# Values of a third token block by Strassen's scheme, and the projections of all blocks made ahead of the three value blocks

## The chip, the core and the metric

The kernel runs on one core of one Trainium2 chip. Its time is the device time of one execution in microseconds. The median of three runs of the kernel before is 831.18 us (830.96 to 831.95). One execution was also taken with the hardware profiler; all views of the profile below come from that one.

## The reference

A block over 2048 tokens of 640 features: layer norm, then on the normalised input both an attention with 32 heads of 20 features and a sliding window of 256 tokens, and a two-layer network with squared ReLU whose output gates the attention's through SiLU. Everything is float32.

```
def _A_ref(x, wqkv, wo):                      # S = 2048, D = 640, H = 32, Dh = 20, W = 256
    qkv = (x @ wqkv).reshape(B, S, 3, H, Dh) ...
    q, k, v = qkv[0], qkv[1], qkv[2]
    scores = einsum("bhqd,bhkd->bhqk", q, k) * Dh ** -0.5
    mask = (i - j >= 0) & (i - j < W)
    p = softmax(where(mask, scores, -1e9))
    o = einsum("bhqk,bhkd->bhqd", p, v)
    return o.reshape(B, S, D) @ wo
def _B_ref(x, w1, b1, w2, b2):                # F = 1536
    h = relu(x @ w1 + b1) ** 2
    return h @ w2 + b2
xn = layernorm(x)
return x + _A_ref(xn, wqkv, wo) * silu(_B_ref(xn, w1, b1, w2, b2))
```

## The kernel before, in words

**Two halves.** Every operand of a large product is kept as two tiles, a high part in the format that TensorE takes (`F32R`) and a low part, the rest. A product then costs three matmuls per chunk of 128: high by high, low by high, high by low. ScalarE (ACT) makes the high part with a copy, VectorE (DVE) or GpSimd (POOL) the low part with a subtraction; in the code the pair is `split`, lines L117 and L118, or `split_w`, L192 and L193.

**Two phases.** Phase 1 (from L428) works on `NB = 4` blocks of `BT = 512` tokens. For each block `b` it normalises x (`norm_jobs`: statistics L157 and L158, the root on ACT L161, four normalisations L166), turns it on TensorE (`transpose_chunks`, 20 transposes L181 into five banks of PSUM, each split into `xT[0][b]` and `xT[1][b]`, the high and the low part), makes the first 128 rows of q and k from it (`qk_group`, 15 matmuls of 512 columns each, L214; `qk_evac` splits the result into `shm` and `slo` and queues their stores to `k_d` and `q_d` in HBM), and makes the values v. The two halves of a block's xT are also copied out whole to `xs` in HBM (`spill_x`, L175), because phase 2 reads them from there again. Phase 2 (the loop `for s in range(steps)` near the end of the file) is attention head pair by head pair, with the remaining projections and the two-layer network filling TensorE between. It begins with the scores of pair 0 (`sps`, L650) on the tiles `ks` and `qs`, which `pair_loads` reads back from `k_d` and `q_d` (L570).

**Values in two ways.** `v_all(b)` makes v of a block directly: 2 halves of the features by 4 tiles of tokens by 15 matmuls of 320 columns, 120 in all (L239). `v_blocks(b)` makes it by Strassen's scheme (in Winograd's form) on pairs of token tiles: two rounds `r`, each with 54 matmuls of the same width (L362, L407, L417, L419), 108 in all. For that it needs sums of the weights, made once (`weight_sums`: four tiles t1 to t4, cut into halves by eight jobs in the list `more`, L302 on ACT and L303 on POOL), and per round sums of the tokens (`token_sum`, kinds k = 1 to 4, on POOL, tile `sx`; `token_round` splits each into `svh` on ACT, L336, and `svl` on DVE, L337). `first_rounds` prepares the first round. Before the change block 0 and block 1 go through `v_all`, blocks 2 and 3 through `v_blocks`.

**Leaving PSUM.** A round has four results. ACT copies a partial product into a tile `m` (L379, three buffers), DVE adds it to a second one and writes v into the tile `vt` (L384). `vt` has two buffers, and a block uses both, one for each half of the features; each is stored to `v_d` in HBM when its block is done, so the first result of the next block has to wait for the store of the block before.

**What sets the order.** Phase 1 is under a manual schedule: on each of the five engines the instructions stand in the order in which the code emits them, and each waits only for its own semaphores. All DMAs of the kernel but a last few are issued by SyncE (SP), in order, on one queue (q1 in the profile). They use eight semaphores in turn, so a DMA cannot be issued before the eighth one back has landed. `store_all` issues what has been collected in `stores`.

Of the kernel before, what the change touches and what calls it, by code (L numbers as in the profile page):

```python
# [24 lines left out]
NB = 4  # L25
# [41 lines left out]
def attn_mlp_kernel(ctx: ExitStack, tc, x, wqkv, wo, w1, b1, w2, b2, out):  # L67
# [74 lines left out]
    with tc.tile_pool(name="ph1v", bufs=2) as p1v, tc.tile_pool(name="ph1", bufs=2) as p1, tc.tile_pool(name="ph1x", bufs=4) as p1b, tc.tile_pool(name="ph1w", bufs=1) as p1w, tc.tile_pool(name="ph1t", bufs=2, space=PSUM) as p1t:  # L142
# [98 lines left out]
        def v_all(b, between=None, firsts=()):  # L241
            jobs = norm_jobs(b + 2) if b + 2 < NB else []
            for nh in range(2):
                if nh and between:
                    between()
                vt = p1v.tile([P, NP // 2, 4, 2, VW], F32, tag="vt", name="vt")
                nc.gpsimd.memset(vt[:, :, :, :, VW - 1:VW], 1.0)
                ahead = 4 if between and not nh else 1
                pss = []
                for t in range(4):  # L250
                    if t in (0, ahead) or t > ahead:
                        ts = range(t, max(t + 1, ahead))
                        for t_ in ts:
                            pss.append(po_.tile([P, BT], F32, tag="o", name="vps")[:, :HALF] if t_ == 3 < ahead else mm_bank([P, HALF], "vps"))
                        for cs in ((range(KC - 1), (KC - 1,)) if len(ts) > 1 else (range(KC),)):
                            for t_, ps in zip(ts, pss):
                                v_part(ps, b, t_, nh, [(xp, wp, c) for c in cs for xp, wp in ((0, 0), (1, 0))], first=not cs[0])
                        for t_, ps in zip(ts, pss):
                            v_part(ps, b, t_, nh, [(0, 1, c) for c in range(KC)], last=True)
                    if firsts and not nh and not t:  # L260
                        firsts[0]()
                    ps = pss.pop(0)
                    psv = ps.rearrange("p (a h d) -> p a h d", a=NP // 2, h=2)
                    dst = vt[:, :, t, :, :]
                    if t % 2:
                        nc.scalar.activation(dst[:, :, :, 0:DH], psv, AF.Copy)
                    else:
                        nc.vector.tensor_copy(dst[:, :, :, 0:DH], psv)
                    if not nh and 0 < t < len(firsts):
                        firsts[t]()  # L270
                    for _ in range(0 if between and not nh else 2 if between else 1):
                        if jobs:
                            jobs.pop(0)()
                    for _ in range(2 if more and b else 0):
                        more.pop(0)()
                    store_all()
                stores.append((v_d[:, nh * (NP // 2):(nh + 1) * (NP // 2), b, :], vt.rearrange("p a t h w -> p a (t h w)")))

        TOKENS = [(b, r) for b in range(2, NB) for r in range(2)]
        sv = [p1w.tile([P, n, P], F32R, name=f"sv{q}{k}") for q in "hl" for k, n in enumerate((2, 2, 3, 2))]  # L280
        sx, sums_t = {}, {}

# [28 lines left out]
        def token_sum(n, k):  # L311
# [2 lines left out]
            (h0, h1), (l0, l1) = [[f32(v) for v in vs] for vs in token_views(n)]  # L314
            one, two = slice(0, 2), slice(3, 5)
            x = sx[k] = p1w.tile([P, 3 if k == 3 else 2, P], F32, tag=f"sx{k}", name=f"sx{k}")
            add, sub = nc.gpsimd.tensor_add, nc.gpsimd.tensor_sub
            if k == 1:
                add(x, h1[:, one], h1[:, two])
                add(x, x, l1[:, one])  # L320
# [108 lines left out]
        with tc.manual_schedule(engines={E_.PE, E_.Activation, E_.DVE, E_.Pool, E_.SP}):  # L429
# [99 lines left out]
            for b in range(NB):  # L529
                def next_x():  # L530
                    if b + 1 < NB:
                        alloc_x(b + 1)
                        transpose_chunks(b + 1, xns)
                        xns.clear()
                        store_all()
                        spill_x(b + 1)

                if b == 0:
                    xns, raws = [], []
# [6 lines left out]

                    def loads1():
                        load_x(2)
                        spill_x(0)
                        nc.sync.dma_start(b1t, b1.rearrange("(c p) -> p c", p=P))  # L550
                        nc.sync.dma_start(b2t, b2.partition_broadcast(P))
                        ones_rows(0)
                        raws.extend(load_w(group_src(1, w), KC) for w in "qk")
                    v_all(b, next_x, [lambda: norm1(0, 4), lambda: None, loads1])
                    more.extend(weight_sums())
                    continue
                for w in "kq":
                    ps = mm_bank([P, BT], "qkps")
                    qk_group(w, b, ps)
                    qk_evac(w, b, ps)  # L560
                    if b == 2:
                        first_rounds(w == "q")
                next_x()
                if b == 2:
                    first_rounds(2)
                if b == NB - 1:
                    store_all()
                    for half in range(2):
                        for dst, src in pair_loads(0, half):
                            nc.sync.dma_start(dst, src)  # L570
                if b == 1:
                    v_all(b)
                    for k in (1, 2, 4, 3):
                        token_sum(0, k)
                else:
                    v_blocks(b)
            store_all()


# [942 lines left out]
```

## Time and profile before

| what | value |
| --- | --- |
| median of the runs | 831.18 us |
| the profiled execution | 831.43 us |
| its span in the profile | 829.7 us |
| busy: TensorE (PE), DVE, ACT, POOL | 99%, 55%, 51%, 44% of the span |
| block 0: values from, to | 18.71, 38.51 us, with the transposes of block 1 inside |
| block 1: q and k; transposes of block 2; values | 38.51; 45.37; 47.47 to 65.16 us |
| block 2: q and k; transposes of block 3; values | 65.16; 72.02; 74.12 to 90.04 us |
| block 3: q and k; values | 90.04; 96.87 to 112.79 us |
| phase 2 on TensorE | from 112.79 us |

A row of the timeline gives the start, the busy time, the engine, the line, the operation with its output and inputs, and how many instructions were merged into it; SPq is the queue of DMA issues on SP. Matmuls are pipelined, so the busy time of a merged row runs a little past the start of the next, and the time of one matmul is best taken from start to start. A row of the windows gives busy time and count of each engine, then the granted clock, the share of the DMA engines and their GB/s.

### The profile page before, as it was taken

How to read it: one execution, taken by the hardware profiler on the slowest of the kernel's cores; microseconds unless marked ns; L12 is line 12 of the kernel's file. 1: busy time of each engine (PE TensorE's matmuls, PEld its weight loads, DVE VectorE, ACT ScalarE, POOL GpSimd, SP SyncE). 2: the span in 40 equal slices, each digit the busy share in tenths (PEclk: the TensorE clock that was granted, in tenths of full speed). 3: DMA queues.
4: the chain of work that ended last, by engine and by line, in shares of the span. 5: the costliest groups of instructions: out<-in, count | busy, mean ns of one | idle time of the engine just before them, and what ended most of it. 6: DMA issues, size and time to landing. Idle time of an engine off the chain costs nothing.

```text
span 829.7 us, 24649 instructions
## 1 busy us (share of the span) xinstructions
PE 822.3 (99%) x10082; PEld 777.8 (94%) x10082; DVE 456.8 (55%) x1398; ACT 425.2 (51%) x760; POOL 361.6 (44%) x672
## 2 busy tenths in 40 slices
PE   8999999999999999999999999999999999999997
PEld 8999999998889999999999999999999999999997
DVE  7856447655577545445444476655455445246663
ACT  6253323556566754743753764844644744754221
POOL 5167900334343543543543543643533643542452
PEclk9999999999999999999999999999999999999999
DMA  6998578888798646446083545585275456345962
GB/s 238 317 396 332 175 205 268 244 274 263 246 312 275 163 149 183 125 160 175 22 262 129 132 118 175 148 245 174 51 241 160 128 186 216 94 132 193 371 264 80
DMA packets 88808, 166.36 MB, mean 201 GB/s; under 512 B 10232, under 2 KB 36472, under 8 KB 87672
## 3 DMA queue, kind: packets, MB, share of 16 engines
q1 hardware_dynamic: 88536, 164.63, 62.7%
q8 instruction: 79, 1.29, 0.7%
q14 instruction: 33, 0.27, 0.1%
q10 hardware_dynamic: 160, 0.16, 0.1%
HBM read 93.66 MB, written 70.52 MB: 198 GB/s over the span
## 4 chain that ended last, share of the span: by engine, by line
PE 97%; DVE 1%; ACT 1%; DMA 0%; issue 0%; ACTq 0%
PE yps L640 21%; PE hps L640 20%; PE qkps L640 14%; PE ops L731 10%; PE wops L800 9%; PE stps L690 5%; PE sps L650 5%; PE vps L239 4%; PE qkps L214 3%; PE vps L362 3%; PE tps L181 1%; PE vps L417 0%; PE vps L407 0%; DMA xt<-in_A_x_dram 0%; DVE st L157 0%; DVE w L1006 0%
## 5 line engine op out<-in xcount | busy, mean ns | idle before, releaser
L658 DVE CUSTOM_DVE_ANT_0 junk<-sps,mask 128x384 bf16<-128x384 f32 (+2 forms) x512 | 252.1, 530 | 256.6 <-PE sps L650 108.2
L696 ACT ACTIVATE p<-stps 128x768 f32<-128x768 f32 (+2 forms) x256 | 197.5, 771 | 248.9 <-PE stps L690 231.4
L697 POOL TENSOR_SCALAR_AFFINE_SELECT p<-p 128x256 f32<-128x256 f32 x256 | 107.8, 421 | 331.6 <-ACT p L696 329.1
L640 PE MATMUL yps<-w,hh 64*128 64x320 f32 x1536 | 225.1, 309 | 0.3 <-DVE ysb L1200 0.2
L640 PE MATMUL hps<-xb,w 64*128 64x256 f32 (+1 forms) x2100 | 210.9, 304 | 0.0
L640 PEld LDWEIGHTS hps<-xb,w 64*128 64x128 f32 x2100 | 196.8, 186 | 3.3 <-issue 2.7
L640 PEld LDWEIGHTS yps<-w,hh 64*128 64x128 f32 x1536 | 185.9, 185 | 3.6 <-issue 2.3
L640 PE MATMUL yps<-w,hl 64*128 64x320 f32 x768 | 175.7, 308 | 0.0
L650 PE MATMUL sps<-ks,qs 60*128 60x384 f32 (+2 forms) x512 | 129.6, 333 | 0.1
L690 PE MATMUL stps<-qs,ks 62*128 62x384 f32 (+2 forms) x512 | 127.3, 331 | 0.2 <-ACT p L696 0.2
L640 PEld LDWEIGHTS yps<-w,hl 64*128 64x128 f32 x768 | 117.8, 185 | 0.4 <-issue 0.4
L640 PE MATMUL qkps<-xT,wgqh 64*128 64x512 f32 x320 | 99.4, 391 | 0.0
L640 PE MATMUL qkps<-xT,wgkh 64*128 64x512 f32 x320 | 98.1, 391 | 0.0
L699 POOL TENSOR_SCALAR_AFFINE_SELECT p<-p 128x256 f32<-128x256 f32 x224 | 94.9, 424 | 0.0
L731 PE MATMUL ops<-p,vp 128*21 128x128 f32 (+1 forms) x2128 | 86.6, 311 | 0.0
L731 PEld LDWEIGHTS ops<-p,vp 128*21 128x21 f32 x2128 | 63.6, 101 | 21.1 <-issue 6.4
L690 PEld LDWEIGHTS stps<-qs,ks 62*128 62x128 f32 x512 | 82.1, 187 | 1.2 <-ACT p L696 0.6
L650 PEld LDWEIGHTS sps<-ks,qs 60*128 60x128 f32 x512 | 81.2, 185 | 2.1 <-DVE mt L658 0.5
L1170 POOL TENSOR_TENSOR hl<-sq,hh 128x512 fp32r<-128x512 f32 x48 | 62.6, 1303 | 16.2 <-ACT sq L1169 15.5
L800 PE MATMUL wops<-wo,oT 128*128 128x320 f32 (+2 forms) x384 | 62.0, 310 | 0.0
L640 PE MATMUL qkps<-xT,wgql 64*128 64x512 f32 x160 | 61.3, 390 | 0.0
L640 PE MATMUL qkps<-xT,wgkl 64*128 64x512 f32 x160 | 61.2, 392 | 0.0
(163 smaller groups left out, 1236.0 us busy)
## 6 DMA issues: line engine op xcount, KB each, us to landing
ks<-k_d SPq DMA_DIRECT2D x64, 240.0 KB
qs<-q_d SPq DMA_DIRECT2D x64, 240.0 KB
xb<-xs SPq DMA_DIRECT2D x60, 256.0 KB
k_d<-shm SPq DMA_DIRECT2D x20, 512.0 KB
q_d<-shm SPq DMA_DIRECT2D x20, 512.0 KB
xs<-xT SPq DMA_DIRECT2D x8, 1280.0 KB
y<-ysb SPq DMA_DIRECT2D x28, 320.0 KB
o<-osb SPq DMA_DIRECT2D x64, 128.0 KB
```

Source lines behind the costliest of these rows:

```text
L214: nc.tensor.matmul(ps, wt[:, c, :], xT[part][b][:, c * BT + t0:c * BT + t0 + n], start=m == 1, stop=m == 3 * KC)
L239: nc.tensor.matmul(ps, xT[xp][b][:, c * BT + t * P: c * BT + (t + 1) * P], wv[wp][:, c, nh * HALF:(nh + 1) * HALF], start=first and m == 0 ...
L640: return nc.tensor.matmul(out, a[r], b_[r], skip_group_check=True, **kw)
L650: nc.tensor.matmul(ss[hh][:, :nk], qs[i][o, q * P:(q + 1) * P], ks[i][o, k0 * P:k0 * P + nk], start=True, stop=True)
L658: nc.vector.tensor_tensor_reduce(out=junk[:, :nk], in0=ss[hh][:, :nk], in1=mask[:, 3 * P - nk:], scale=1.0, scalar=-3.0e38, op0=ALU.add, o ...
L690: nc.tensor.matmul(tps[:, hh, :n], ks[i][o, kb * P:(kb + 1) * P], qs[i][o, kb * P:kb * P + n], start=True, stop=True)
L696: nc.scalar.activation(p32[:, :, :n], tps[:, :, :n], AF.Exp, scale=SCALE)
L697: nc.gpsimd.affine_select(p32[:, :, 0:P], p32[:, :, 0:P], pattern=[[0, 2], [1, P]], compare_op=ALU.is_ge, fill=0.0, base=0, channel_multip ...
L699: nc.gpsimd.affine_select(p32[:, :, 2 * P:], p32[:, :, 2 * P:], pattern=[[0, 2], [-1, P]], compare_op=ALU.is_gt, fill=0.0, base=0, channel ...
L731: nc.tensor.matmul(ot[r0:r0 + VW, c0:c0 + len(part), :], vps[p][:, kb // 4, kb % 4, hh, :], pts[p, kb][:, hh, :].rearrange("p (t n) -> p t ...
L800: nc.tensor.matmul(ps, a, b_, start=j == 0, stop=j == n - 1)
L1170: nc.gpsimd.tensor_sub(hh[1][:, :BT], sq, f32(hh[0]))
```

## The change

Block 1's values are now made by `v_blocks` too, so the list of rounds, `TOKENS`, has six entries in place of four. The order of phase 1 becomes: q and k of block 1, transposes of block 2, q and k of block 2, transposes of block 3, q and k of block 3, and then `v_blocks` of blocks 1, 2 and 3 in a row. The normalisation of block 3 (`norm_jobs(3)`), which was spread over `v_all(1)`, now follows the transposes of block 2. The jobs that cut the weight sums, also spread over `v_all(1)`, are taken three at a time behind each evacuation of q or k. The token sums of kind 3 go from POOL to DVE; those of the first round stand between k and q of block 2. `spill_x` leaves its four places, and all four blocks' copies are issued together at the start of block 3. The reads of `ks` and `qs` for pair 0 come before the three value blocks and not before the last one.

```
@@ v_all
-                    for _ in range(2 if more and b else 0):
-                        more.pop(0)()
                     store_all()
@@
-        TOKENS = [(b, r) for b in range(2, NB) for r in range(2)]
+        TOKENS = [(b, r) for b in range(1, NB) for r in range(2)]
@@ token_sum
-            add, sub = nc.gpsimd.tensor_add, nc.gpsimd.tensor_sub
+            eng = nc.vector if k == 3 else nc.gpsimd
+            add, sub = eng.tensor_add, eng.tensor_sub
@@ the loop over blocks
                         transpose_chunks(b + 1, xns)
                         xns.clear()
                         store_all()
-                        spill_x(b + 1)
...
                         load_x(2)
-                        spill_x(0)
...
                     more.extend(weight_sums())
                     continue
+                if b == NB - 1:
+                    for b_ in range(NB):
+                        spill_x(b_)
                 for w in "kq":
                     ps = mm_bank([P, BT], "qkps")
                     qk_group(w, b, ps)
                     qk_evac(w, b, ps)
-                    if b == 2:
+                    for _ in range(min(3, len(more))):
+                        more.pop(0)()
+                    if b == 2 and w == "k":
+                        for k in (1, 2, 4, 3):
+                            token_sum(0, k)
+                    if b == NB - 1:
                         first_rounds(w == "q")
                 next_x()
-                if b == 2:
-                    first_rounds(2)
-                if b == NB - 1:
-                    store_all()
-                    for half in range(2):
-                        for dst, src in pair_loads(0, half):
-                            nc.sync.dma_start(dst, src)
                 if b == 1:
-                    v_all(b)
-                    for k in (1, 2, 4, 3):
-                        token_sum(0, k)
-                else:
-                    v_blocks(b)
+                    for job in norm_jobs(NB - 1):
+                        job()
+            first_rounds(2)
+            store_all()
+            for half in range(2):
+                for dst, src in pair_loads(0, half):
+                    nc.sync.dma_start(dst, src)
+            for b in range(1, NB):
+                v_blocks(b)
             store_all()
```

The change shifts the lines behind it by one or two (the cut on ACT is L302 before and L300 after, the addition into `vt` L384 and L383). Three places of the order, each as the engine's instructions stand, show what moves.

ACT from the evacuation of block 1's k and q to the transposed halves of block 2 (`shm` is the high part of k or q, `t1h` to `t3h` are cut weight sums, `xT_2` the high half of block 2); before:

```order
L117 ACTIVATE shm<-qkps 128x512 x2
L117 ACTIVATE xT_2_707<-tps 128x512 x5
L302 ACTIVATE t3h<-wvr_195 128x320 x2
L266 ACTIVATE vt<-vps 128x8x2x20
L302 ACTIVATE t1h<-wvr_194 128x320 x2
L302 ACTIVATE t2h<-wvr_194 128x320 x2
```

and now:

```order
L117 ACTIVATE shm<-qkps 128x512
L300 ACTIVATE t3h<-wvr_195 128x320 x2
L300 ACTIVATE t1h<-wvr_194 128x320
L117 ACTIVATE shm<-qkps 128x512
L300 ACTIVATE t1h<-wvr_194 128x320
L300 ACTIVATE t2h<-wvr_194 128x320 x2
L117 ACTIVATE xT_2_715<-tps 128x512 x5
```

Three cuts now stand between the evacuation of q and the five copies of block 2's halves, which came directly behind each other before.

DVE from the low halves of block 2 to those of block 3, now (`st`, `mv`, `rstd` and `xn` are the statistics and the normalised x of block 3, `slo` the low parts of block 2's k and q, `sx_819` the first round's token sum of kind 3); the statistics of the other three tiles are left out, and before, these lines stood between the additions and copies of block 1's values:

```order
L118 TENSOR_TENSOR xT_2_716<-tps,xT_2_715 128x512 x5
L157 BN_STATS st<-xt_0_639 128x6 x2
L158 BN_AGGR mv<-st 128x2
...
L162 RECIPROCAL rstd<-rstd 128x4
L166 TENSOR_SCALAR xn<-xt_0_639,mv,rstd 128x640
...
L166 TENSOR_SCALAR xn<-xt_3_645,mv,rstd 128x640
L118 TENSOR_TENSOR slo<-qkps,shm 128x512
L325 TENSOR_TENSOR sx_819<-xT_1_505 128x384
L326 TENSOR_TENSOR sx_819<-sx_819,xT_1_506 128x384
L327 TENSOR_TENSOR sx_819<-sx_819,xT_1_506 128x384
L118 TENSOR_TENSOR slo<-qkps,shm 128x512
L118 TENSOR_TENSOR xT_3_844<-tps,xT_3_843 128x512 x5
```

The whole normalisation of block 3 stands between the halves of block 2 and the evacuation of block 2's k, and three token sums between the evacuations of k and q.

SP from the last store of block 2's q to the first stores of v, now (`xs` are the copies of x, `ks` and `qs` the reads for pair 0; rows that repeat for the other half are left out):

```order
L206 DMA q_d<-slo 128x512
L175 DMA xs_0_72<-xT_0_182 128x2560
L175 DMA xs_0_76<-xT_0_183 128x2560
...
L175 DMA xs_3_75<-xT_3_843 128x2560
L175 DMA xs_3_79<-xT_3_844 128x2560
L206 DMA k_d<-shm 128x2x512
...
L206 DMA q_d<-slo 128x512
L576 DMA ks_117<-k_d 60x1024
...
L576 DMA qs_116<-q_d 60x1024
L206 DMA v_d<-vt 128x8x168 x6
```

Before, two of the eight `xs` copies stood in each block's turn, and the stores of v of a block came ahead of the next block's q and k.

## The prediction

> **What bounds the kernel now.** I read the page's busy times first, then the chain that ended last, then TensorE's timeline over the stage that the change rewrites.
>
> ```profile
> span 829.7 us, 24649 instructions
> PE 822.3 (99%) x10082; PEld 777.8 (94%) x10082; DVE 456.8 (55%) x1398; ACT 425.2 (51%) x760; POOL 361.6 (44%) x672
> PE 97%; DVE 1%; ACT 1%; DMA 0%; issue 0%; ACTq 0%
> ```
>
> TensorE is the bound, with almost no idle time: 97% of the chain is its own work. A matmul taken away is worth its time, and every wait that TensorE gets is added in full, since nothing later is idle that could absorb it. So the stage decides.
>
> ```profile
> 45.37 2.34 PE L181 MATMUL tps<-ident,xn 128*128 128x128 f32 x20
> 47.47 17.85 PE L239 MATMUL vps<-wv,xT 128*128 128x320 f32 x120
> 65.16 1.33 PE L214 MATMUL qkps<-xT,wgkh 128*128 128x512 f32 x5
> 66.33 1.32 PE L214 MATMUL qkps<-xT,wgkl 128*128 128x512 f32 x5
> 72.02 2.35 PE L181 MATMUL tps<-ident,xn 128*128 128x128 f32 x20
> 74.12 2.45 PE L362 MATMUL vps<-wv,xT 128*128 128x320 f32 x15
> 90.04 1.32 PE L214 MATMUL qkps<-xT,wgkh 128*128 128x512 f32 x5
> ```
>
> From start to start: 20 transposes 2.10 us (45.37 to 47.47), direct values of a block 17.69 (to 65.16), q and k 6.86 (to 72.02), Strassen values 15.92 (74.12 to 90.04). The reader should see the order as well: behind the transposes of block 2 stand 17.69 us of values of block 1, which need nothing new. That is the cover under which ACT and DVE finish block 2's halves, normalise block 3 and cut the weight sums, and under which the queue writes x out.
>
> **The gain.** 108 matmuls for 120, at 17.69 / 120 = 15.92 / 108 = 0.147 us each: 12 x 0.147 = 1.8 us off. It is all that the change removes from TensorE; transposes, q and k stay.
>
> **Term 1: the halves of block 2.** Now q and k of block 2 follow its transposes, so they wait for ACT's copies.
>
> ```profile
> 45.62 0.60 ACT L117 ACTIVATE shm<-qkps 128x512 fp32r<-128x512 f32 x1 [2.80 <-PE qkps L214]
> 46.11 2.55 ACT L117 ACTIVATE xT<-tps 128x512 fp32r<-128x512 f32 x5
> 52.63 1.50 ACT L302 ACTIVATE t1h<-wvr 128x320 fp32r<-128x320 f32 x2
> 54.01 1.51 ACT L302 ACTIVATE t2h<-wvr 128x320 fp32r<-128x320 f32 x2
> ```
>
> The five copies began 0.49 us behind the evacuation of q and ended at 48.66. Three cuts now stand in between, at (54.01 - 52.63) / 2 = 0.69 each, 2.1 us: the fifth copy ends at 50.75. The fifth matmul of k would start at 47.47 + 4 x 0.234 = 48.4 (0.234 is (66.33 - 65.16) / 5) and now starts at 50.8: a wait of 2.4 us, and q of block 2 ends at 47.47 + 6.86 + 2.4 = 56.7. The cuts before q's evacuation are hidden, as ACT idled 2.80 us there.
>
> **Term 2: the normalisation of block 3.** Its cover has shrunk from 17.69 us to the 6.86 of q and k, and it begins late.
>
> ```profile
> 46.86 3.07 DVE L118 TENSOR_TENSOR xT<-tps,xT 128x512 fp32r<-128x512 f32 x5
> 54.76 0.88 DVE L157 BATCH_NORM_STATS2 st<-xt 128x6 f32<-128x320 f32 x2
> 55.80 0.83 DVE L157 BATCH_NORM_STATS2 st<-xt 128x6 f32<-128x320 f32 x2
> 38.07 0.30 ACT L161 ACTIVATE rstd<-mv,eps 128x4 f32<-128x4 f32 x1 [3.33 <-DVE mv L158]
> 38.61 2.18 DVE L166 TENSOR_SCALAR xn<-xt,mv,rstd 128x640 f32<-128x640 f32 x4
> 61.88 1.63 DVE L166 TENSOR_SCALAR xn<-xt,mv,rstd 128x640 f32<-128x640 f32 x2
> L118 DVE TENSOR_TENSOR slo<-qkps,shm 128x512 fp32r<-128x512 f32 x6 | 4.1, 689 | 12.8 <-ACT shm L117 12.8
> L337 DVE TENSOR_TENSOR svl<-sx,svh 128x384 fp32r<-128x384 f32 x4 | 2.4, 588 | 0.5 <-ACT svh L336 0.5
> L337 DVE TENSOR_TENSOR svl<-sx,svh 128x256 fp32r<-128x256 f32 x12 | 9.4, 787 | 5.2 <-ACT svh L336 5.2
> 70.10 0.41 DVE L337 TENSOR_TENSOR svl<-sx,svh 128x256 fp32r<-128x256 f32 x1
> ```
>
> DVE's low halves of block 2 follow the copies by one subtraction: 50.75 + 0.7 = 51.45. Statistics of a tile take 55.80 - 54.76 = 1.04, of four 4.2: 55.6. Root and reciprocal take 0.55 (38.07 to 38.61): 56.15. Four normalisations take 2.2 us with POOL idle (the row at 38.61) and 2 x 1.63 = 3.3 with POOL busy (61.88): 58.3 to 59.4. TensorE has run out at 56.7. Its transposes can then go, but k of block 3 needs the PSUM bank that q of block 2 leaves, and that evacuation stands behind the one of k (0.69) and behind three token sums which are new on DVE. No row has them there; the nearest is the subtraction of the same width, 0.59, and for the dear end I add what POOL's company costs the narrower one, 0.787 against 0.41 at rest: 0.97. So 0.69 + 3 x 0.59 + 0.69 = 3.15, or 4.3: k of block 3 starts at 61.4 to 63.7, middle 62.5, where without waits it would start at 47.47 + 6.86 + 2.10 = 56.4. Terms 1 and 2 together: **6.1 us (5.0 to 7.3)**. The 20 transposes end by 61.5 and lie inside this; so do block 3's copies.
>
> The Trainium skill ("SBUF — State Buffer", section "Who interferes with whom") says that a DVE operation with two SBUF inputs and a POOL operation lock each other out for whole instructions; taking a POOL token sum's length as a full wait would lift the three sums further, and is a rival below.
>
> **Term 3: v of block 1 leaves late.** All eight copies of x now go to the queue when q of block 2 has been stored, just ahead of everything else.
>
> ```profile
> xs<-xT SPq DMA_DIRECT2D x8, 1280.0 KB
> v_d<-vt SPq DMA_DIRECT2D x8, 672.0 KB
> q_d<-shm SPq DMA_DIRECT2D x6, 512.0 KB
> ks<-k_d SPq DMA_DIRECT2D x6, 240.0 KB
> 41.71 4.85 SPq L149 DMA_DIRECT2D xt<-in_A_x_dram  x4
> 52.07 0.89 DVE L157 BATCH_NORM_STATS2 st<-xt 128x6 f32<-128x320 f32 x2 [1.56 <-DMA xt<-in_A_x_dram]
> 40.00:52.00 12.00, 12.00 (x76) 10.99 (x75) 7.92 (x14) 5.02 (x9) 5.92 (x7) 1.00 1.05 386
> 78.00:82.00 4.00, 4.00 (x30) 4.00 (x29) 2.35 (x5) 1.85 (x5) 3.77 (x5) 1.00 1.04 435
> 94.00:98.00 4.00, 4.00 (x22) 3.49 (x21) 0.99 (x2) 1.20 (x3) 3.77 (x5) 1.00 0.97 332
> 104.00:110.00 6.00, 6.00 (x43) 6.00 (x42) 3.48 (x8) 2.23 (x6) 0.24 (x1) 1.00 0.91 203
> 114.00:118.00 4.00, 4.00 (x26) 3.47 (x26) 0.95 (x7) 0.00 (x0) 0.00 (x0) 1.00 0.96 300
> 113.00 2.68 SPq L206 DMA_DIRECT2D v_d<-vt  x2
> 118.45 0.34 SPq L591 DMA_DIRECT2D vp<-v_d  x1
> ```
>
> The queue is served in order: the tiles of x issued from 41.71 on came only at 52.07, after 12 us at 386 GB/s, as much as the copies of x ahead of them hold. Its rates by stage are 435 GB/s (copies of x), 332 (stores of q and k), 203 (the reads for pair 0), 300 (v). Ahead of the first v store of block 1, counted from T = the start of k of block 3: 0.8 us until data flows (two v stores are 1.38 MB, 4.6 us at 300, and took 113.00 to 118.45), the last store of q 0.8, eight copies of x 10.49 MB / 435 = 24.1, q and k of block 3 1.57 MB / 332 = 4.7, eight reads 1.97 MB / 203 = 9.7, the store itself 0.69 MB / 300 = 2.3: it lands at T + 42.4.
>
> Who waits: block 2's first result, since `vt` has two buffers, and DVE stands behind it; the second round's `svl` is made there. TensorE goes on through k and q (6.86), block 1 (15.92), one round (7.96) and 15 matmuls (2.2) to T + 32.9, then needs it. DVE has it one addition (0.5) and one subtraction (0.41 to 0.79) after the landing, at T + 43.4: 10.4 us. Neither ACT nor anything else on TensorE fills this, as orders are fixed. The second half of `vt` is free 2.3 us later, and with it the tile `m` for the next copy; TensorE has nine matmuls (1.3 us) until it needs that: 0.95 more. After such a pause TensorE may be slow again, as it was at the start:
>
> ```profile
> 1.74 4.95 PE L434 MATMUL warm_ps<-ident 128*128 128x128 f32 x22 [1.74 <-POOL ident L100]
> 7.59 1.25 PE L481 MATMUL warm_ps<-ident 128*128 128x128 f32 x10
> ```
>
> 22 transposes took 4.95 us where ten took 1.25 a little later (22 x 0.11 = 2.4): 0 to 2.5 us, partly under the 0.95. I take 1.7 for both and **12.0 us** for term 3. The ends: everything at 435 GB/s lands at T + 36.2 with DVE, 3.3 us; copies of x at the 386 of 40:52 and the whole cold start, 10.4 + 3.1 + 2.5 = 16. The row at 52.07 speaks against an earlier landing, so no lower end than that is taken into the term.
>
> The Trainium skill ("TensorE: Matmul & The Clock Gate", Part 1) puts the cold stretch at about 3.4 us of half rate after an idle window of that length, which would cost 1.7; no row here shows a pause in mid-run.
>
> **Costed at nothing.** Block 3 waits for block 2's stores likewise, but the queue is empty by then and the two stores of 113.00 landed within 5.4 us, less than the 8 us until TensorE notices. The reads for pair 0 land some 24 us before the scores. POOL makes 42 token sums in six rounds where it made 40 in four, and stays under the rounds. x of block 3 is loaded earlier than before, no `xs` ahead of it.
>
> **Sum.** The profiled execution took 831.4 (0.2 over the median of the runs): 831.4 - 1.8 + 6.1 + 12.0 = 847.7; I say **847.5**. Own range: 831.4 - 1.8 + 5.0 + 3.3 = 838 to 831.4 - 1.8 + 7.3 + 16 = 853.
>
> **Rivals.** *The v store is not late* (landed before T + 33, because the queue overtakes or moves x faster): terms 1 and 2 alone, 831.4 - 1.8 + 6.1 = 835.7. For it: SP has issued the reads early. Against it: 15.0 MB in the 32 us after the first data would need 469 GB/s throughout, and even the copies of x went at 435. 10%.
>
> *Faster: DVE keeps up.* The place is the fourth normalisation of block 3; if it is done when TensorE ends q of block 2, and the v store is in time, only the 12 matmuls are left: 829.6. It decides from 54.3 on. Against it: 4.2 + 0.55 + 2.2 = 6.95 us of DVE work begin at 49.93 at the earliest (46.86 + 3.07). 3%.
>
> *DVE becomes the bound of the rounds.* Per round it has four results (0.5 each), four subtractions, now three sums: 2.0 + 1.8 + 1.8 = 5.6 us of TensorE's 7.96, and with POOL's company 2.0 + 3.0 + 2.9 = 7.9. If each sum waits for a whole POOL sum, about 0.4 us more each, a round takes 9.1, and the four rounds of blocks 1 and 3 lose 1.1 each: 852. 9%. The rule of the Trainium skill on the shared lock speaks for this one.
>
> That the change makes fewer matmuls is seen in the order; it cannot fail to do that.
>
> **How the numbers follow.** The forecast has 78%. The range of 838 to 853 holds nearly all of it and the last rival; to reach 8 in 10 safely it goes down to 836, the edge of the first rival. What this kernel's measurement can tell from no change is about 0.2%, 1.7 us: faster 0.03, the same 0.02, slower 0.95.
>
> **What would show it.** In the changed profile TensorE's timeline: a gap of about 2.4 us behind 47.47, one of 3 to 5 before k of block 3, ended by DVE, and one of about 10 in the second round of block 2, ended by DVE, whose first `vt` addition there waits for a DMA `v_d`. The copies of x should fill the queue for 24 us without a break. It would be wrong if block 2 ran its two rounds without a gap, or if the gaps before it came to less than 4 us.

## The result, and the profile after

The changed kernel takes 851.37 us (median; 851.18 to 851.52) where the kernel before, on the same chip, takes 831.07 (830.85 to 831.95): a ratio of 1.0244, with a 95% interval of 1.0229 to 1.0259. The change removes 12 matmuls and costs 20.3 us. The forecast was 847.5 with a range of 836 to 853.

The page of the kernel after: span, busy times with their instructions, the granted clock in 40 slices, and the chain that ended last.

```profile
span 849.7 us, 24678 instructions
PE 823.8 (97%) x10070; PEld 776.9 (91%) x10070; DVE 478.0 (56%) x1428; ACT 429.9 (51%) x772; POOL 364.0 (43%) x674
PEclk9999889999999999999999999999999999999999
PE 89%; DMA 5%; DVE 3%; ACT 1%; SPq 1%; issue 1%; DVEq 0%; ACTq 0%
```

TensorE has 10070 matmuls for 10082, so the saving was made. But its share of the chain fell from 97% to 89%, and the two slices in which the clock is not whole (85 to 127 us) say where to look. TensorE's timeline after, the rows with a wait in phase 1 (the wait and what ended it stand in brackets), and the start of block 2's q:

```profile
49.23 2.45 PE L214 MATMUL qkps<-xT,wgkh 128*128 128x512 f32 x5 [1.10 <-ACT xT L117]
53.82 1.29 PE L214 MATMUL qkps<-xT,wgqh 128*128 128x512 f32 x5
57.65 0.76 PE L181 MATMUL tps<-ident,xn 128*128 128x128 f32 x2 [0.27 <-DVE xn L166]
59.31 0.33 PE L181 MATMUL tps<-ident,xn 128*128 128x128 f32 x1 [0.90 <-DVE xn L166]
60.54 2.07 PE L181 MATMUL tps<-ident,xn 128*128 128x128 f32 x17 [0.90 <-DVE xn L166]
64.30 1.39 PE L214 MATMUL qkps<-xT,wgkh 128*128 128x512 f32 x5 [1.69 <-DVE slo L118]
109.65 0.64 PE L361 MATMUL vps<-t1h,svl 128*128 128x320 f32 x1 [12.18 <-DVE svl L336]
```

These are the three places that the prediction named: k of block 2 waits for ACT's copies (49.23), block 3's transposes and its k wait for DVE (57.65 to 64.30), and the second round of block 2 waits 12.18 us for its `svl`. The queue's issues and DVE behind that last wait:

```profile
64.57 9.78 SPq L175 DMA_DIRECT2D xs<-xT  x8
99.44 34.96 SPq L206 DMA_DIRECT2D v_d<-vt  x6
108.77 0.49 DVE L383 TENSOR_TENSOR vt<-vps,m 128x320 f32<-128x320 f32 x1 [16.49 <-DMA v_d<-vt]
```

The first store of block 1's values is issued only at 99.44, 34.9 us behind the first of the eight copies of x, and DVE stands idle 16.49 us for its landing.

The sum from rows: this execution runs 0.4 us later than the one before from the start (k of block 1 at 38.91, not 38.51). k of block 3 starts at 64.30, where without waits it would have started at 56.4 + 0.4 = 56.8: 7.5 us for terms 1 and 2. Block 3's values follow 53.0 us later (117.3), against 6.86 + 2 x 15.92 = 38.7 without a wait: 14.3 us for term 3. Together 7.5 + 14.3 - 1.8 = 20.0, against 20.0 between the two profiled executions (851.43 and 831.43) and 20.3 between the medians.

### The profile page after: what moved, and what is told of

Its sections match the earlier page's. It is cut to its first block, busy times and chain, and to the rows that moved or that the text cites. A ratio compares the mean times of both kernels' runs of the same rounds, so it can differ in the third digit from the quotient of the medians.

```text
span 849.7 us, 24678 instructions
## 1 busy us (share of the span) xinstructions
PE 823.8 (97%) x10070; PEld 776.9 (91%) x10070; DVE 478.0 (56%) x1428; ACT 429.9 (51%) x772; POOL 364.0 (43%) x674
## 4 chain that ended last, share of the span: by engine, by line
PE 89%; DMA 5%; DVE 3%; ACT 1%; SPq 1%; issue 1%; DVEq 0%; ACTq 0%
PE yps L642 21%; PE hps L642 20%; PE qkps L642 14%; PE ops L733 10%; PE wops L802 8%; PE stps L692 5%; PE sps L652 5%; PE vps L239 2%; PE vps L361 2%; DMA ks<-k_d 2%; DMA xs<-xT 2%; PE qkps L214 1%; DMA v_d<-vt 1%; DVE st L157 1%; DVE xn L166 1%
## 5 line engine op out<-in xcount | busy, mean ns | idle before, releaser
L699 POOL TENSOR_SCALAR_AFFINE_SELECT p<-p 128x256 f32<-128x256 f32 x256 | 107.8, 421 | 331.3 <-ACT p L698 327.3
```

Of the source, the lines that this page charges most:

```text
L699: nc.gpsimd.affine_select(p32[:, :, 0:P], p32[:, :, 0:P], pattern=[[0, 2], [1, P]], compare_op=ALU.is_ge, fill=0.0, base=0, channel_multip ...
```

## The experiments

Each run changes the kernel after, unless another is named, and is timed beside the kernel before on the same chip (831.0 to 831.1 us each time). The cuts of code show the main lines of each edit, not all of it.

### Copies of x at their old places

```
@@ next_x
                         store_all()
+                        spill_x(b + 1)
@@ loads1
                         load_x(2)
+                        spill_x(0)
@@ the loop over blocks
-                if b == NB - 1:
-                    for b_ in range(NB):
-                        spill_x(b_)
```

> The changed kernel (851.4 us), with only the eight copies of x put back to the four places they had before (block 0's behind the loads of block 2's x, the others behind their block's transposes). Theory (the first v store of block 1 lands late because everything ahead of it in the queue has to go first): 7.9 MB less stands ahead of it, it lands some 18 us earlier and before TensorE needs it, the 12.2 us gap in block 2 and the 2.2 us of slow clock behind it go: 851.4 - 14.4 = 837.0. Rival 1 (the gap comes from the order of issues on SP, whose stores of k, q and v all wait for each other, and not from bytes): 851, unchanged. Rival 2 (the copies of block 1 now stand before the loads of block 3's x and make its normalisation late): the block 2 gap goes, but the one before block 3's q and k grows by up to 3 us: 840.

Measured: 836.97 us (836.23 to 837.25), ratio 1.0069 [1.0052, 1.0085]. The wait in block 2 is gone: one order on the queue cost 14.4 us, as much as the rows gave for term 3 (14.3). What remains is terms 1 and 2, with one thing added: the rows of x for block 3 come late behind the copies, the second rival of the expectation in small. DVE's first statistics of block 3, TensorE's transposes and k of that block, and a window of 2 us (busy time of PE, PEld, DVE, ACT, POOL, then clock, DMA share, GB/s):

```profile
52.87 0.89 DVE L157 BATCH_NORM_STATS2 st<-xt 128x6 f32<-128x320 f32 x2 [1.00 <-DMA xt<-in_A_x_dram]
58.44 0.76 PE L181 MATMUL tps<-ident,xn 128*128 128x128 f32 x2 [1.49 <-DVE xn L166]
59.39 0.33 PE L181 MATMUL tps<-ident,xn 128*128 128x128 f32 x1 [0.20 <-DVE xn L166]
59.91 3.74 PE L181 MATMUL tps<-ident,xn 128*128 128x128 f32 x17 [0.19 <-DVE xn L166]
64.54 1.40 PE L214 MATMUL qkps<-xT,wgkh 128*128 128x512 f32 x5 [0.89 <-DVE slo L118]
60.00:62.00 2.00, 2.00 (x11) 2.00 (x12) 1.94 (x3) 2.00 (x4) 1.25 (x1) 0.52 1.00 423
```

The 17 transposes take 3.74 us where they took 2.07 in the kernel after, at a clock of 0.52: TensorE slowed down here behind waits of 1.5 us and less. That slow clock cost no time, though: k of block 3 behind the transposes still waits 0.89 us for DVE, whose chain of statistics, normalisations and token sums sets its start.

### Reads for pair 0 behind block 1's values

```
-            for half in range(2):
-                for dst, src in pair_loads(0, half):
-                    nc.sync.dma_start(dst, src)
             for b in range(1, NB):
                 v_blocks(b)
+                if b == 2:
+                    for half in range(2):
+                        for dst, src in pair_loads(0, half):
+                            nc.sync.dma_start(dst, src)
```

> The changed kernel with the eight reads of ks and qs for pair 0 put behind the v stores of block 1 (after the second Strassen block), all else the same. Theory (bytes ahead in one queue): 2 MB of reads at 203 GB/s, 9.7 us, leave the path of the v store, the gap in block 2 shrinks from 12.2 to about 2.5 us and the clock stays up: 851.4 - 9.7 - 2.2 = 839.5. Rival (only the copies of x count, because the reads end on other partitions and run beside the stores): 851. If the reads come too late for the scores, the start of phase 2 shows a gap on DMA.

Measured: 842.45 us (840.78 to 843.7), ratio 1.0136 [1.0119, 1.0152]: 8.9 us less than the change, but 3 more than expected. TensorE's rows in block 2 (the profiled execution, at 843.7 us, is the slowest of the four):

```profile
99.66 0.41 PE L361 MATMUL vps<-t1h,svl 128*128 128x320 f32 x1 [2.59 <-DVE svl L336]
102.16 0.63 PE L361 MATMUL vps<-t2h,svh 128*128 128x320 f32 x1 [1.07 <-ACT m L378]
```

The wait fell by 9.6 us, the time of the reads, as term 3 has it (9.7). What the expectation lacked is the second wait, of 1.07 us, and the clock: behind the first wait it stood at one half from 101.0 to 107.8, some 3 us of work lost (the rows stand in the last section).

### Statistics of block 3 earlier

```
                     qk_evac(w, b, ps)
+                    if b == 1 and w == "k":
+                        jobs3 = norm_jobs(NB - 1)
+                        for job in jobs3[:3]:
+                            job()
+                    elif b == 1:
+                        for job in jobs3[3:5]:
+                            job()
@@ behind the transposes of block 2
-                    for job in norm_jobs(NB - 1):
+                    for job in jobs3[5:]:
```

> The changed kernel with the statistics of block 3 (four tiles, 4 us on DVE) between the evacuations of block 1's k and q and right behind that of q, where DVE waits anyway, and not behind block 2's halves. Theory (DVE's chain of statistics, root, normalisation sets the start of block 3's q and k, and all later waits count from there): 851.4 - 4.0 = 847.4, with the gap in block 2 still 12 us. Rival 1 (the landing of the v store hangs on something that started earlier, so the gap in block 2 grows by what is saved): 851. Rival 2 (k and q of block 2 end only at 57.2, so only part of the 4 us can be saved before another wait shows): 849.

Measured: 846.13 us (845.33 to 849.8), ratio 1.019 [1.0167, 1.0212]: 5.2 us less, about all of term 2. Its TensorE and DVE:

```profile
59.47 2.35 PE L181 MATMUL tps<-ident,xn 128*128 128x128 f32 x20
53.17 2.18 DVE L166 TENSOR_SCALAR xn<-xt,mv,rstd 128x640 f32<-128x640 f32 x4
107.06 0.63 PE L361 MATMUL vps<-t1h,svl 128*128 128x320 f32 x1 [11.97 <-DVE svl L336]
```

All 20 transposes go without a wait, and the wait in block 2 stays: the two are separate costs. The four normalisations took 2.18 us here, with POOL done before them. These rows are from the slowest of the four executions (849.8 us): in it the clock stood at one half from 51.8 to 55.2 as well, which drew out the matmuls for k of block 2 by some 1.5 us. An execution near the median was not profiled.

### Cuts behind block 2's copies

```
-                    for _ in range(min(3, len(more))):
+                    for _ in range(min(3, len(more)) if (b, w) != (1, "q") else 0):
                         more.pop(0)()
@@ behind the transposes of block 2
                 if b == 1:
+                    for _ in range(3):
+                        more.pop(0)()
```

> The changed kernel with the three cuts that stand behind the evacuation of block 1's q put behind the copies of block 2's halves. Theory (the three cuts delay ACT's copies by 2.1 us, and with them q and k of block 2 and the normalisation of block 3): 851.4 - 2.1 = 849.3; the first gap on TensorE of about 2.5 us falls to 0.4. Rival (the wait for block 3's normalisation takes up what the first gap gives back): 851, with the second gap longer by 2 us.

Measured: 849.41 us (848.96 to 850.71), ratio 1.0223 [1.0208, 1.0238]: 2.0 us less, against the 2.4 of term 1. Its k of block 2:

```profile
47.59 1.75 PE L214 MATMUL qkps<-xT,wgkh 128*128 128x512 f32 x5
```

The wait of 1.10 us ahead of it is gone (in the kernel after it started at 49.23), and its five matmuls take 1.75 for 2.45. What came of it later is seen at k of block 3 and at the wait in block 2:

```profile
62.05 2.47 PE L214 MATMUL qkps<-xT,wgkh 128*128 128x512 f32 x5 [0.82 <-DVE slo L118]
107.23 0.63 PE L361 MATMUL vps<-t1h,svl 128*128 128x320 f32 x1 [10.10 <-DVE svl L336]
```

K of block 3 starts 2.25 us earlier than after the change, but then runs at half clock (2.47 us for 1.39), and the values of block 1 start only 0.3 us earlier (70.89 for 71.22), as this whole execution does. The gain comes back at the wait in block 2, 10.10 for 12.18: the copies of x were issued at 62.32 for 64.57, and the first addition of block 2 that waits for the store follows this issue by 44.0 us here and by 44.2 in the kernel after (44.4 with the statistics early). So while the store of block 1's values is late, a wait in phase 1 costs time because it delays the queue, and not by the time that TensorE itself loses there.

### Values of block 2 collected in another room

```
-                vts.append(p1v.tile([P, NP // 2, 4, 2, VW], F32, tag="vt", name="vt"))
...
+                if b == 2:
+                    vts.append(xT[nh][0][:, :NP // 2 * 4 * 2 * VW].rearrange("p (a t h w) -> p a t h w", a=NP // 2, t=4, h=2))
+                else:
+                    vts.append(p1v.tile([P, NP // 2, 4, 2, VW], F32, tag="vt", name="vt"))
...
```

Left out are the column of ones, which POOL copies into the new place, and the type under which the values are stored. This kernel no longer gives the block's output; it serves only to time the wait.

> The changed kernel, queue and order as they are, but block 2's values are collected in the room of block 0's transposed x, which is free by then, and not in the two buffers that wait for block 1's store (block 2's values are thereby rounded to the format of TensorE's operands). Theory (the late v store reaches TensorE only through the wait for a free buffer): the store lands as late as before, some 44 us after block 3's k begins, but nothing in block 2 waits; block 3, which now takes block 1's buffers, begins its results about then; 851.4 - 14.4 = 837.0. Rival (the full queue holds TensorE by another way as well, the stores' tiles or the reads for pair 0): 840 or more, with a gap on DMA elsewhere.

Measured: 836.38 us (836.17 to 836.94), ratio 1.0065 [1.0052, 1.0079]. The queue is as full as after the change, and still 15.0 us are gone: the late store costs only because the next block's first result needs its buffer. Here that wait falls on block 3's first result, and it has shrunk to a length that TensorE does not notice:

```profile
108.61 0.49 DVE L390 TENSOR_TENSOR vt<-vps,m 128x320 f32<-128x320 f32 x1 [1.00 <-DMA v_d<-vt]
```

### All four remedies together

The copies of x go to their old places, but block 1's behind the loads of block 3's rows; statistics early; cuts later; the first sum of kind 3 behind q of block 2 and no longer behind its k.

```
@@ the loop over blocks
                     v_all(b, next_x, [lambda: norm1(0, 4), lambda: None, loads1])
+                    spill_x(1)
...
-                    if b == 2 and w == "k":
-                        for k in (1, 2, 4, 3):
+                    if b == 2:
+                        for k in (1, 2, 4) if w == "k" else (3,):
                             token_sum(0, k)
```

> The change with its waits taken away: the copies of x in their old places, except that block 1's stand behind the loads of block 3's x; block 3's statistics between the evacuations of block 1's k and q; the three cuts behind block 2's copies; the first round's token sum of kind 3 behind the evacuation of block 2's q. Theory (three waits, each of its own cause, cost 2.5 + 4.9 + 14.4 us, and the 12 matmuls bring 1.8): all three go but for some tenths, 831.1 - 1.8 + 0.5 = 829.8, faster than before by 0.15%. Rival 1 (the waits hand on to each other: with the copies early, block 3's x or the stores of k and q become late): 832 to 835. Rival 2 (DVE, with three more sums per round, bounds the six rounds): gaps of 0.5 to 1 us in each round, 834.

Measured: 835.99 us (835.86 to 836.83), ratio 1.0062 [1.0049, 1.0075]. The expected 829.8 was missed by 6 us, and its rows show the first rival of the expectation, and a second loss:

```profile
50.71 2.89 PE L214 MATMUL qkps<-xT,wgkh 128*128 128x512 f32 x5
61.27 0.69 DVE L118 TENSOR_TENSOR slo<-qkps,shm 128x512 fp32r<-128x512 f32 x1 [2.41 <-DMA q_d<-slo]
62.11 1.53 PE L214 MATMUL qkps<-xT,wgkh 128*128 128x512 f32 x5 [2.10 <-DVE slo L118]
71.65 2.36 PE L361 MATMUL vps<-wv,xT 128*128 128x320 f32 x15
...
111.21 2.36 PE L361 MATMUL vps<-wv,xT 128*128 128x320 f32 x15
```

The copies of x now stand in front of the stores of block 1's q; its buffer `slo` comes free late, block 2's evacuation of q waits for it, and k of block 3 for the PSUM bank (2.10 us). The second loss is in k of block 2: its third group takes 2.89 us where 1.30 is usual, as DVE makes the low halves that it reads only from 50.02 to 53.05, behind the statistics of four tiles. In the three Strassen blocks nothing is left: five rounds in 111.21 - 71.65 = 39.56 us, 7.91 each, the pace of the kernel before (15.92 / 2).

### Sums of kind 3 back on POOL

In the kernel with all remedies, and in the kernel after:

```
-            eng = nc.vector if k == 3 else nc.gpsimd
+            eng = nc.gpsimd
```

> As the run with all waits taken away, but with the token sums of kind 3 on POOL as before the change. POOL then has ten sums in each round, 8.5 us by the rows of the kernel before, where TensorE needs 7.96. Theory (the move to DVE was needed, since POOL falls behind by half a microsecond in each of six rounds): svl comes late in the last rounds, 1 to 3 us slower than the run beside it. Rival (POOL's lead of a round and a half covers it): the same as that run, 829.8, or a little faster since DVE has less to do.

> The changed kernel with only the token sums of kind 3 back on POOL. Theory (three sums on DVE, 0.54 + 0.98 + 0.96 in the trace, stand between the evacuations of block 2's k and q, and block 3's k waits for the second): k of block 3 starts 2.4 us earlier, 851.4 - 2.4 = 849.0, the gap in block 2 stays 12 us, which also hides POOL's longer rounds. Rival (the bank is not what block 3's k waits for, the transposed halves are): 851.

Measured: with all remedies 841.64 us (839.83 to 843.19), ratio 1.0127 [1.0113, 1.0141], 5.6 us slower than with the sums on DVE; in the kernel after 852.64 (852.14 to 854.18), ratio 1.0266 [1.025, 1.0281], 1.3 slower where 2.4 faster was expected. With all remedies, TensorE's last wait and POOL's first sum of two rounds in a row:

```profile
111.66 0.42 PE L361 MATMUL vps<-t2h,svh 128*128 128x320 f32 x1 [1.93 <-ACT m L378]
91.17 0.72 POOL L318 TENSOR_TENSOR sx<-xT 128x256 f32<-128x256 f32 x1
100.50 0.72 POOL L318 TENSOR_TENSOR sx<-xT 128x256 f32<-128x256 f32 x1
```

A round of ten sums takes POOL 100.50 - 91.17 = 9.3 us, more than the 7.91 that TensorE needs for it. POOL was busy for 16.9 of the 18 us from 91 to 109, so with six rounds in a row it becomes the bound. In the kernel after with this edit:

```profile
61.91 1.70 PE L214 MATMUL qkps<-xT,wgkh 128*128 128x512 f32 x5
108.93 0.63 PE L361 MATMUL vps<-t1h,svl 128*128 128x320 f32 x1 [13.11 <-DVE svl L336]
121.68 0.41 PE L361 MATMUL vps<-t2h,svh 128*128 128x320 f32 x1 [1.71 <-ACT m L378]
```

K of block 3 did start earlier, at 61.91 for 64.30, of which 0.5 is the earlier start of that execution; but the wait in block 2 is 13.11 for 12.18, and there is a new one of 1.71 in block 3, which fits sums that come late from POOL. So the move of these sums to DVE, which costs 1.9 us ahead of block 3's k, is needed for the rest of the change.

### Where can 10 MB stand on one queue?

Three kernels looked for an order of the copies in which nothing that TensorE soon needs stands behind them. All have the cuts later and, unlike the one with all remedies, the statistics of tiles 2 and 3 behind block 2's copies.

First, block 0's copies at their old place, those of blocks 1 and 2 behind the stores of their own k and q, block 3's behind the reads for pair 0, and the first sum of kind 3 behind q of block 2:

```
@@ next_x
                         store_all()
+                        if b:
+                            spill_x(b)
@@ ahead of v_blocks
+            spill_x(NB - 1)
```

> The change with four of its orders altered: the copies of x back stand at block 0's old place, for block 1 behind the stores of block 1's k and q, for block 2 behind those of block 2's k and q, for block 3 behind the reads for pair 0; only tiles 0 and 1 of block 3 have their statistics early (behind block 1's k), tiles 2 and 3 behind block 2's copies; the three cuts stand behind block 2's copies; the first sum of kind 3 stands behind block 2's q. If the 4.8 us by which the earlier kernel with all the places stayed behind the kernel before were the stores of k and q late behind the copies of x, and block 2's low halves late behind statistics, both are gone: no wait of TensorE over 1.5 us before the values and none over 0.6 in them, no clock under 0.8 after 55 us, and 829.5 to 832 (before: 831.0). Rival: the normalisations of block 3 behind block 2's copies and the first cut beside them still make the transposes of block 3 wait, with a clock of 0.5 or 0.6 there: 832.5 to 836.

Measured: 834.92 us (834.67 to 836.5), ratio 1.0042 [1.0028, 1.0056]. The rows of x for block 3 come late, behind block 0's copies, and with them DVE's statistics and block 1's q:

```profile
47.44 0.89 DVE L157 BATCH_NORM_STATS2 st<-xt 128x6 f32<-128x320 f32 x2 [3.71 <-DMA xt<-in_A_x_dram]
50.27 2.47 PE L214 MATMUL qkps<-xT,wgkh 128*128 128x512 f32 x5 [2.63 <-DVE slo L118]
```

Neither theory of the expectation had this wait: the stores were in time, and the place of the loss moved forward. Second, block 0's copies behind those loads, and the first sum of kind 3 behind block 3's low halves:

```
                     load_x(b + 1)
+                    spill_x(0)
@@ behind the transposes of block 3
+                if b == 2:
+                    token_sum(0, 3)
```

> The kernel with the copies of x back behind the stores, with two further orders altered: block 0's copies back stand behind the loads of block 3's rows of x (there the rows landed at 47.4 us, and statistics that waited for them held up block 1's last evacuation of q: TensorE waited 2.63 us at 50.3 us and then ran some 1.6 us slower), and the first sum of kind 3 stands behind block 3's low halves (there it held them up by 1.5 us). If these were what is left, the rows land before 45 us, the wait at 50 us falls to 1.2 or less with the clock whole behind it, and the kernel takes 830.0 to 832.0 (before: 831.1; the one before this: 834.9). Rival: the clock falls at the transposes of block 3 anyway, or the stores of block 1's k and q, now 6 us later, hold up block 2's evacuation: 832.5 to 835.

Measured: 840.02 us (839.45 to 840.95), ratio 1.0105 [1.0088, 1.0122], worse than before the edit and than the rival's 832.5 to 835. The rows of x landed in time (no wait at 50 us), but now the stores are late, and ACT waits 3.79 us for one of block 1's k:

```profile
56.01 0.60 ACT L117 ACTIVATE shm<-qkps 128x512 fp32r<-128x512 f32 x1 [3.79 <-DMA k_d<-shm]
59.34 2.43 PE L214 MATMUL qkps<-xT,wgkh 128*128 128x512 f32 x5 [0.86 <-DVE slo L118]
97.70 0.63 PE L362 MATMUL vps<-t1h,svl 128*128 128x320 f32 x1 [3.38 <-DVE svl L337]
```

and the last row is term 3 again, in small: block 1's value stores behind block 3's copies. Third, block 0's copies stand behind the stores of block 1's k and q, and the others go into the Strassen rounds: those of blocks 1 and 2 behind block 1's value stores, block 3's behind block 2's:

```
@@ v_blocks, behind its store_all
+                if not r:
+                    for b_ in {2: (1, 2), 3: (3,)}.get(b, ()):
+                        spill_x(b_)
@@ next_x
-                        if b:
-                            spill_x(b)
+                        if b == 1:
+                            spill_x(0)
```

> The kernel before this one (block 0's copies back behind the loads of block 3's rows) with the copies of x back placed where nothing that TensorE soon needs stands behind them: block 0's behind the stores of block 1's k and q, those of blocks 1 and 2 behind block 1's value stores, those of block 3 behind block 2's value stores. If late stores were the whole remainder (in the last run the waits of 1.22 and 0.86 us behind k and q at 57 to 59 us, the wait of 3.38 us in the values of block 2, and some 4 us at a lower clock behind them), no wait over 1.5 us is left from 38 to 118 us, and the kernel takes 829.5 to 831.5 (before: 831.1). Rival: the values' stores of block 2, now behind 5 MB, are late for block 3's collection, a wait of 1 to 4 us there with a slower clock: 832.5 to 836.

Measured: 830.97 us (830.69 to 832.05) against 831.1 (830.72 to 833.0) for the kernel before: a ratio of 0.9999 [0.9989, 1.0008]. All 20 us are back, and 830.97 is as fast as the kernel before and no faster. Its TensorE rows (k of block 2, the transposes and k of block 3) and the issues of the copies of blocks 1 and 2:

```profile
47.34 1.75 PE L214 MATMUL qkps<-xT,wgkh 128*128 128x512 f32 x5
56.07 2.07 PE L181 MATMUL tps<-ident,xn 128*128 128x128 f32 x17 [0.90 <-DVE xn L166]
57.90 1.70 PE L214 MATMUL qkps<-xT,wgkh 128*128 128x512 f32 x5
82.34 5.21 SPq L175 DMA_DIRECT2D xs<-xT  x4
```

The wait of 0.90 and the two first groups of k, which take 0.4 us more each than behind values (1.75 and 1.70 against 1.33, since they follow ACT's copies closely), make 1.7 us: what the 12 matmuls save. Without the cover of block 1's values, ACT's five copies and DVE's four normalisations show on TensorE, and that price equals the gain. A version that beats the kernel before was not found; keeping POOL quiet during those normalisations, which could take the 0.90 away, was not tried.

## Why the prediction was right

**The gain** was right: 12 matmuls, 1.8 us.

**Term 1** (halves of block 2): 2.4 forecast. ACT's copies stood behind the three cuts as computed, and q of block 2 started at 53.82, where 45.37 + 0.4 + 2.10 + 3.43 = 51.3 was free of waits: 2.5 us; taking the cuts away gave 2.0. Right.

**Term 2** was mis-sized: terms 1 and 2 together 7.5 us for 6.1, just above the upper bound of 7.3. The steps on DVE in the kernel after:

```profile
56.89 3.59 DVE L166 TENSOR_SCALAR xn<-xt,mv,rstd 128x640 f32<-128x640 f32 x4
61.01 0.54 DVE L325 TENSOR_TENSOR sx<-xT 128x384 f32<-128x384 f32 x1
61.58 0.98 DVE L326 TENSOR_TENSOR sx<-sx,xT 128x384 f32<-128x384 f32 x1
62.59 0.96 DVE L327 TENSOR_TENSOR sx<-sx,xT 128x384 f32<-128x384 f32 x1
```

The prediction put four normalisations at 2.2 to 3.3 us and took the middle; beside POOL's cuts they took 3.59 (2.18 in the run with the statistics early, with POOL at rest), and they began 0.3 later. The first two took 0.57 us each, the third and fourth 1.24 and 1.30, when POOL's cuts had begun (57.88). The three sums took 2.48, of the 1.77 to 2.9 allowed: 0.54 for the one that began between two operations of POOL, 0.98 and 0.96 for the two that began inside one. The rule of the Trainium skill on the shared lock ("SBUF — State Buffer", "Who interferes with whom") agrees with these pairs, 0.54 against 0.98 and 2.18 against 3.59: DVE's operation became longer where POOL's ran beside it. I should have taken the dear end for the normalisations, since POOL has work at that time in the changed order.

**Term 3**, the v of block 1 that leaves late, was right in mechanism and place. Three runs each take away a different link: without the copies ahead of the store (14.4 us less) or the buffer that waits for it (15.0 less) the wait of TensorE is gone, and without the reads ahead of it (8.9 less) it shrinks from 12.18 to 2.59. Its size was 14.3 to 15.0 for 12.0, inside its 3.3 to 16. The landing was 2.1 us later than T + 42.4 (at 108.8 with T = 64.3). Some 1.0 of that is the rate of the copies' 10.49 MB, taken at 435 GB/s and measured thus (last figure of the row):

```profile
66.00:84.00 18.00, 18.00 (x112) 17.09 (x111) 13.88 (x22) 7.06 (x18) 11.97 (x16) 1.00 1.01 417
```

The rest lies in the stores and reads behind them and was not resolved further. TensorE waited 12.18 us, not 10.4, and lost 2.0 us to the slow clock behind it, where 1.7 had been taken for clock and tile `m` together.

**The rivals.** That the store would not be late is excluded by the wait of 16.49 us on DVE; that DVE keeps up, by the waits for `xn`. That DVE becomes the bound of the rounds fell with the run of all remedies: five rounds at 7.91 us each, DVE's three sums among them. The shared lock lengthens single operations, but a round has room for it.

**Costed at nothing.** Block 3's wait for block 2's stores and the reads for pair 0 cost nothing visible, as said. POOL "stays under the rounds" held only because three of its ten sums a round went to DVE.

## What to carry to other kernels

A queue that is served in order is a resource of the critical path, even where no transfer on it is urgent: before moving megabytes on it, list what is issued behind them for the next 40 us, which buffer each of those frees, and which engine's next instruction needs that buffer. The work that a block hides is a cost of removing or moving that block: here 17.7 us of plain matmuls were the cover for ACT's copies, DVE's normalisations and one block's share of the 10 MB of stores, and with the best order found a saving of 1.8 us was spent on what came out from under them. Where TensorE is the bound, short waits close together should be added up, and can cost more than their length, as the next section shows.

## What the runs showed of the hardware

I had expected a slow clock after a pause of 10 us, and not after waits of 1 to 2.6. Windows of 0.25 us, two each of the kernel after, of the one with late reads for pair 0, and of the one with the copies at their old places (the clock is the third figure from the end):

```profile
100.00:100.25 0.25, 0.00 (x0) 0.00 (x0) 0.00 (x0) 0.00 (x0) 0.00 (x0) 0.60 0.99 246
113.50:113.75 0.25, 0.25 (x2) 0.25 (x2) 0.25 (x1) 0.15 (x1) 0.17 (x2) 0.59 0.00 0
```

```profile
100.75:101.00 0.25, 0.25 (x3) 0.08 (x1) 0.00 (x0) 0.00 (x0) 0.00 (x0) 0.96 0.53 115
107.75:108.00 0.25, 0.25 (x3) 0.25 (x2) 0.25 (x2) 0.00 (x0) 0.05 (x1) 0.88 0.95 180
```

```profile
60.00:60.25 0.25, 0.25 (x2) 0.25 (x3) 0.23 (x1) 0.25 (x1) 0.00 (x0) 0.65 0.90 377
63.25:63.50 0.25, 0.25 (x3) 0.04 (x1) 0.25 (x1) 0.25 (x2) 0.25 (x2) 0.52 1.26 532
```

Between each pair the clock is 0.50. A window of 0.60 is whole for a fifth and half for the rest, so the clock fell at 100.05 and came back at 113.70: 13.65 us. In the same way the second pair gives 100.98 to 107.81, 6.83 us, and the third 60.08 to 63.49, 3.41 us. These are four, two and one times 3.41. The Trainium skill ("TensorE: Matmul & The Clock Gate", Part 1) describes a free-running window of 3413 ns by which activity is judged, and the lengths agree with it. What its table names as the condition, an idle window, was not needed: in the 3.41 us before the third fall TensorE's waits come to 1.9 us (1.49, 0.20 and 0.19), and the rest was work. How much waiting is enough was not measured: in the kernel after, a wait of 1.69 us (at 64.30) brought no fall. A fall costs up to 1.7 us of work for each such window, half of 3.41, and all of that where the window is full of work: in the second and the third case, some 2.9 us (half of 6.83 less the wait of 1.07) and 1.7 (3.74 less 2.07). Whether the time pays for it hangs on what TensorE waits for next. In the second case nothing follows that waits, and the loss is nearly as much again as the waits around it (3.7); in the third it is hidden, as k of block 3 still waits for DVE. The windows do not start with the kernel: counted from the starts of their kernels, the falls at 100.05 and 100.98 are no multiple of 3.41 apart. So the same waits can bring it about in one execution and not in the next. That this is the spread of 3 to 4.5 us which the kernels with late reads and with early statistics show is argued, not shown, since only one execution of each was profiled.
